# Two buffers for raw weight blocks, conversions stored from their own buffer, gate values turned on TensorE, and larger packets for operands kept in DRAM

## The chip, the cores and the metric

The kernel runs on one core of one Trainium2 chip. The metric is device time in microseconds (us), the median of several executions. All times of single instructions come from one profiled execution.

## What is computed

The reference, cut to what matters here (inputs are float32, the two matrices of the last layer float64):

```python
x = attention(q, k, v, s)          # causal, with a bias from cumsum(max(s, 0)); x is [2304, 512]
P = exp(x @ w_gate - max)          # [2304, 8 experts]
for _ in range(8):                 # rows and columns scaled in turn
    P /= P.sum(1) + 1e-9; P /= P.sum(0) + 1e-9; P *= 2304 / 8
out = 0
for e in range(8):                 # w1[e] is [512, 1024], w2[e] is [1024, 512]
    out += P[:, e:e+1] * (max(x @ w1[e], 0) @ w2[e])
h = out @ w_in                     # w_in is [512, 2048], w_out [2048, 512]
return max(0.01 * h, h) @ w_out
```

## The kernel before

Attention comes first (to about 201 us). The rest is cut into *units*. A unit takes 256 columns of a layer's first matrix and 256 rows of its second for 768 tokens (two blocks of 384, `W = 384`). The tokens make three passes, j = 0, 1, 2. Each pass has 32 units for the 8 experts (4 units an expert), and after the third come three passes of 8 units for the last layer, 120 units in all. In every unit the first product is done by a scheme with seven block products instead of eight: P1 to P7 (function `product`, lines 288 to 290, six matmuls of 384 columns each, since every operand is split into a high and a low part). The order is P1, P6, P5, P7, P2, P4, P3. P1 and P2 go to the PSUM bank that the profile calls FA.

**Pass j = 0** also makes the operands. For unit n, `weights1` loads a raw block of w1 (512 KB) into the tile RAW1 (a part of RB), GpSimd forms four sums of its blocks (SW, also in RB), ScalarE casts to the high parts, GpSimd subtracts to the low parts, all into WQ, of which there are two sets used in turn. `weights2` does the same with a raw block of w2 (tile RAW2), and `sums` forms four sums for later passes in the tile SS. Everything made is stored in DRAM for passes 1 and 2: `w1c` (1792 KB a unit) and `w2s` (1280 KB a unit). In pass 0 the second product of a unit runs plainly (`second`, 36 matmuls of 512 columns), one unit behind the first. VectorE combines the seven products (L956), makes low parts (L984) and adds into `acc` (L1051).

**Passes j = 1, 2 and the last layer** read the made operands back: `fetch1` loads one of the seven blocks of w1c (256 KB) into one of 11 slots, `fetch2` those of w2s, and the second product uses seven products too.

**The conversion** of the float64 matrices (32 blocks, 19 of them in units 4 to 28 of pass 0, in three units of every four; functions `convert`, `conversion`) loads a block into one of two buffers BITS, takes eight VectorE steps (L929 to L936) through the scratch tiles `cva` and `cvb`, and stores `cva` to DRAM (L948). From 1339 us on, `prepare` makes the last layer's operands out of them. **The gate** values P are made by `gating` in the first units; eight stores `pt<-P` (L1086), one per expert, write them to DRAM in the order [expert, token], for passes 1 and 2.

All DMAs are issued by one queue, SyncE's (SP in the profile), in program order: an issue whose wait is open holds everything behind it. The program order of every engine comes from a planner (class `Flow`): every piece of work is entered by `do(engine, key, duration, emit, reads, writes, latency)`, waits follow from the names read and written, and a list schedule with these numbers sets the order. Before, each DMA is entered with 100 ns on SP and a latency of 2500 to 12000 ns.

Of the kernel before, what the change touches and what calls it, by code (L numbers as in the profile page):

```python
# [113 lines left out]
def fused_kernel(ctx: ExitStack, tc: tile.TileContext, q, k, v, s, w_gate, w1, w2, w_in, w_out, out):  # L114
# [110 lines left out]
    def weights1(do, n, key):  # L225
        s = n % 2
        wa, wb = views(n)
        waf = [x.bitcast(F32) for x in wa]
# [1 line left out]
        A = lambda o, k: RAW1[:, 2 * k:2 * k + 2, 128 * o:128 * o + 128]  # L230
        do("sp", key - 0.6, 100, lambda: nc.sync.dma_start(out=RAW1, in_=w1[e][:, 256 * i:256 * i + 256].rearrange("(c p) f -> p c f", p=128)), [], ["raw1"], 3500)
        do("pool", key, pgg(256), sub(SW[:, 0], A(1, 0), A(1, 1), ALU.add), ["raw1"], ["s1"])
        do("pool", key + 0.01, pgg(256), sub(SW[:, 1], SW[:, 0], A(0, 0), ALU.subtract), ["raw1", "s1"], ["s2"])
        do("pool", key + 0.02, pgg(256), sub(SW[:, 2], A(0, 0), A(1, 0), ALU.subtract), ["raw1"], ["s3"])
# [4 lines left out]
        do("act", key + 0.03, pa(256), lambda: nc.scalar.copy(wa[0][:, 6], A(1, 1)), ["raw1"], [("wh6", s)])
        do("act", key + 0.04, pa(1024), lambda: nc.scalar.copy(wa[0][:, 0:4], SW), ss, [("wh0", s)])  # L240
        do("pool", key + 0.04, pgg(512), sub(wa[1][:, 4:6], left, waf[0][:, 4:6], ALU.subtract), ["raw1", ("wh4", s)], [("wl4", s)])
        do("pool", key + 0.05, pgg(256), sub(wa[1][:, 6], A(1, 1), waf[0][:, 6], ALU.subtract), ["raw1", ("wh6", s)], [("wl6", s)])
        do("pool", key + 0.06, pgg(1024), sub(wa[1][:, 0:4], SW, waf[0][:, 0:4], ALU.subtract), ss + [("wh0", s)], [("wl0", s)])

    def weights2(n, key):

# [4 lines left out]
        do("act", key + 0.5, pa(1024), lambda: nc.scalar.copy(wb[0], RAW2), ["raw2"], [("vh", s)])
        do("pool", key + 0.5, pgg(1024), sub(wb[1], RAW2, wb[0].bitcast(F32), ALU.subtract), ["raw2", ("vh", s)], [("vl", s)])
        do("sp", key + 0.9, 100, lambda: nc.sync.dma_start(out=w1c[n], in_=WQ.bitcast(F32)[:, s, 0:2 * NA]), [(x, s) for x in ("wh0", "wl0", "wh4", "wl4", "wh6", "wl6")], [("w1c", n)], 8000)
        for a in range(2):
# [1206 lines left out]
```

## Time and profile before

| | |
|---|---|
| median of 3 runs | 2232.85 us (2225.61 to 2233.7) |
| the profiled execution, its own time | 2235.46 us |
| its span in the profile | 2233.7 us |
| TensorE busy | 2052.5 us, 92% |
| VectorE, GpSimd busy | 1655.9 us, 74%; 1675.0 us, 75% |
| ScalarE busy | 904.0 us, 40% |
| DMA | 518.24 MB in 411474 packets, 106618 of them under 512 B |
| mean granted TensorE clock | 0.972 of full speed |

The shares are means over stages with different limits; the windows by stage, below, tell them apart. PE is TensorE, DVE VectorE, ACT ScalarE, POOL GpSimd. L231 is line 231 of the kernel.

### The profile page before, as it was taken

What the parts mean: (1) busy time and instruction counts of PE and PEld (TensorE: products, weight loads), DVE (VectorE), ACT (ScalarE), POOL (GpSimd) and SP (SyncE); (2) the same over time, 40 slices, a digit from 0 to 9 for tenths busy, and PEclk for the clock granted to TensorE, in tenths of its full rate; (3) what the DMA queues carried; (4) which work ended last, traced back from release to release, by engine and by line L of the source; (5) the groups of instructions that cost most, each with busy time, mean ns of one, the idle gap of its engine ahead of it and who ended that gap; (6) DMA issues with size and microseconds to landing.
All of it is one profiled execution on the core that took longest, in us unless ns stands there. A gap on an engine that the chain in (4) does not pass through costs nothing. (4 is left out here: it accounts for less than half of the span.)

```text
span 2233.7 us, 35592 instructions
## 1 busy us (share of the span) xinstructions
PE 2052.5 (92%) x11471; PEld 1922.6 (86%) x11471; DVE 1655.9 (74%) x2987; ACT 904.0 (40%) x1895; POOL 1675.0 (75%) x1607
## 2 busy tenths in 40 slices
PE   7999967688888799999999999999999999999998
PEld 5786756577777688999999999999999989999997
DVE  6786547466666676889999889788788886776846
ACT  5887312122222223433333344433333344555553
POOL 7789745466666674888888887788777887888885
PEclk9999988899999999999999999999999999999999
DMA  6654768876667667877877779899889977777673
GB/s 148 141 136 127 273 134 195 185 209 244 254 254 263 240 238 274 256 243 248 252 248 248 231 235 286 273 295 296 291 264 292 291 237 254 227 243 214 213 230 99
DMA packets 411474, 518.24 MB, mean 232 GB/s; under 512 B 106618, under 2 KB 298106, under 8 KB 407194
## 3 DMA queue, kind: packets, MB, share of 16 engines
q1 hardware_dynamic: 411290, 515.98, 74.7%
q8 instruction: 92, 1.51, 0.3%
q14 instruction: 92, 0.75, 0.1%
HBM read 362.11 MB, written 144.04 MB: 227 GB/s over the span
## 5 line engine op out<-in xcount | busy, mean ns | idle before, releaser
L288 PE MATMUL sc<-XO,WQ 128*128 128x384 f32 x960 | 333.6, 347 | 78.4 <-DVE HB L984 42.0
L289 PE MATMUL sc<-XO,WQ 128*128 128x384 f32 x960 | 327.5, 341 | 0.0
L290 PE MATMUL sc<-XO,WQ 128*128 128x384 f32 x960 | 326.2, 340 | 0.0
L288 PEld LDWEIGHTS sc<-XO,WQ 128*128 128x128 f32 x960 | 184.9, 193 | 101.2 <-DVE HB L984 45.7
L1229 DVE TENSOR_TENSOR WQ<-WQ 128x512 fp32r<-128x512 f32 x176 | 190.0, 1080 | 58.1 <-ACT WQ L1228 56.9
L267 POOL TENSOR_TENSOR SS<-RAW 128x256 f32<-128x256 f32 x64 | 51.7, 808 | 221.4 <-DMA RAW<-in_moe_w_dram 221.4
L289 PEld LDWEIGHTS sc<-XO,WQ 128*128 128x128 f32 x960 | 184.6, 192 | 4.6
L290 PEld LDWEIGHTS sc<-XO,WQ 128*128 128x128 f32 x960 | 184.6, 192 | 0.0
L1228 ACT CAST WQ<-WQ 128x512 fp32r<-128x512 f32 x176 | 109.2, 620 | 163.8 <-DMA WQ<-w2s 131.6
L1250 DVE TENSOR_TENSOR X<-tr,X 128x384 f32<-128x384 f32 x275 | 149.9, 548 | 33.9 <-PE tr L1244 33.6
L288 PE MATMUL FA<-XO,WQ 128*128 128x384 f32 x480 | 162.5, 339 | 4.5 <-ACT Up L957 2.3
L290 PE MATMUL FA<-XO,WQ 128*128 128x384 f32 x480 | 161.2, 336 | 0.7 <-POOL WQ L223 0.7
L289 PE MATMUL FA<-XO,WQ 128*128 128x384 f32 x480 | 161.4, 336 | 0.0
L956 DVE TENSOR_TENSOR sc<-sc,Uu 128x384 f32<-128x384 f32 x240 | 133.7, 557 | 30.0 <-PE sc L290 29.3
L223 POOL TENSOR_TENSOR WQ<-RB,WQ 128x512 fp32r<-128x512 f32 (+2 forms) x96 | 143.3, 1509 | 4.0 <-ACT WQ L240 2.7
L1211 POOL TENSOR_TENSOR HB<-GG,HB 128x384 fp32r<-128x384 f32 x96 | 107.9, 1127 | 31.0 <-ACT HB L1210 30.9
L956 DVE TENSOR_TENSOR Uu<-FB,Up 128x384 f32<-128x384 f32 x120 | 65.9, 549 | 70.7 <-ACT Up L957 43.8
L929 DVE TENSOR_SCALAR CV<-CV 128x512 uint32<-128x512 uint32 x32 | 25.9, 810 | 113.1 <-DMA win<-CV 107.9
L223 POOL TENSOR_TENSOR RB<-RB 128x256 f32<-128x256 f32 x128 | 94.7, 759 | 17.7 <-DMA RB<-in_moe_w_dram 16.0
L1243 PE MATMUL tr<-HB,WQ 128*128 128x384 f32 x307 | 103.4, 337 | 1.2 <-POOL HB L1211 1.2
L1242 PE MATMUL tr<-HB,WQ 128*128 128x384 f32 x307 | 103.4, 337 | 0.1
L1034 PE MATMUL Y<-WQ,HB 128*128 128x512 f32 x128 | 55.2, 431 | 52.6 <-DVE acc L1051 51.9
(335 smaller groups left out, 6977.4 us busy)
## 6 DMA issues: line engine op xcount, KB each, us to landing
WQ<-w1c SPq DMA_DIRECT2D x616, 256.0 KB
WQ<-w2s SPq DMA_DIRECT2D x440, 256.0 KB
w1c<-WQ SPq DMA_DIRECT2D x32, 1792.0 KB
RB<-in_moe_w_dram SPq DMA_DIRECT2D x32, 512.0 KB
RAW<-in_moe_w_dram SPq DMA_DIRECT2D x32, 512.0 KB
w2s<-WQ SPq DMA_DIRECT2D x64, 256.0 KB
w2s<-SS SPq DMA_DIRECT2D x32, 512.0 KB
CV<-in_moe_w_in_dram SPq DMA_DIRECT2D x16, 512.0 KB
```

The costliest lines, as they stand in the source:

```text
L223: return lambda: nc.gpsimd.tensor_tensor(out=out, in0=x, in1=y, op=op)
L288: nc.tensor.matmul(t, lhsT=hi, rhs=xh, start=new, stop=False, skip_group_check=on)
L289: nc.tensor.matmul(t, lhsT=hi, rhs=xl, start=False, stop=False, skip_group_check=on)
L290: nc.tensor.matmul(t, lhsT=lo, rhs=xh, start=False, stop=(k == 1), skip_group_check=on)
L956: TT = lambda out, x, y: (lambda: v.tensor_tensor(out=out, in0=x, in1=y, op=ALU.add))
L1034: nc.tensor.matmul(y, lhsT=hh, rhs=wb[0][:, f], start=(f == 0), stop=False)
L1211: do(eng, t + 0.02, pgg(W) if eng == "pool" else pq(W), lambda: (nc.gpsimd if eng == "pool" else nc.vector).tensor_tensor(out=OP[k][:, 1], ...
L1228: do("act", t, pa(512), lambda: nc.scalar.copy(hi, lo.bitcast(F32)), [("w2l", k)], [("w2h", k)])
L1229: do(eng, t + 0.05, pgg(512) if eng == "pool" else pd(512), lambda: (nc.gpsimd if eng == "pool" else nc.vector).tensor_tensor(out=lo, in0= ...
L1242: nc.tensor.matmul(y[:, 0:W], lhsT=hi, rhs=oh, start=(x == 0), stop=False)
L1243: nc.tensor.matmul(y[:, 0:W], lhsT=hi, rhs=ol, start=False, stop=False)
L1250: do("dve", t + 0.08, pq(W), lambda: nc.vector.tensor_tensor(out=a, in0=y[:, 0:W], in1=a, op=ALU.add), [yr], [("A", name, s_)])
```

## The change

1. *Raw blocks.* RAW1 and RAW2 become lists of two. The second RAW1 is the upper half of the tile SS, the second RAW2 the start of the tile PB (which holds gate values in later passes). Unit n uses buffer n mod 2, and the loads are entered 0.7 of a unit earlier. SS, before two buffers for `sums`, becomes one.
2. *Conversions.* The last VectorE step writes into the block's own BITS buffer and the store reads from there, so `cva` is free with that step; the buffer's next load waits for the store.
3. *Gate values.* Two TensorE transposes turn P, ScalarE copies the result to SBUF, and two stores write it as [18 tiles, 9, 128 tokens]; the eight stores L1086 go. Loads of PB read three runs of 128 values for each partition in place of one of 384.
4. *Operands in DRAM.* w2s is laid out by pairs of units so that a fetched block is one run in each partition (2 KB, and 4 KB for the new w2d, which holds high and low parts together, in place of 1 KB pieces). The sums' store then writes 1 KB pieces where it wrote 4 KB. The seven blocks of w1c are reordered so that those of P1, P5, P6, P7 stand together: one fetch of 1 MB (8 KB in each partition) into one of two buffers brings them, the other three come alone, each into one buffer of its own.
5. *Planner.* A DMA is entered with 3.2 ns a KB on SP and a latency of 2000 ns (2500 ns for the gate values).

```diff
-    RAW1 = RBw[:, 0:1024].rearrange("p (c f) -> p c f", c=4)
+    RAW1 = [RBw[:, 0:1024].rearrange("p (c f) -> p c f", c=4)]
...
-        do("sp", key - 0.6, 100, lambda: nc.sync.dma_start(out=RAW1, ...), [], ["raw1"], 3500)
+        do("sp", key - 1.3, kb(512), lambda: nc.sync.dma_start(out=raw, ...), [], [r1], 2000)
...
-        do("sp", key - 0.5, 100, lambda: nc.sync.dma_start(out=RAW2, ...), [], ["raw2"], 3500)
+        do("sp", key - 1.2, kb(512), lambda: nc.sync.dma_start(out=raw, ...), [], [r2], 2000)
...
-        sums(do, n, key + 0.6, RAW2, "raw2", SS[:, n % 2], ("ss", n % 2), "pool")
+        sums(do, n, key + 0.6, raw, r2, SS, "ss", "pool")
...
+    RAW2 = [RAWt, PB_.rearrange("p a b n -> p (a b n)")[:, 0:1024].rearrange("p (c f) -> p c f", c=2)]
+    SS = SSt[:, 0:1024].rearrange("p (k f) -> p k f", k=4)
+    RAW1.append(SSt[:, 1024:2048].rearrange("p (c f) -> p c f", c=4))
...
+        def turn():
+            for h in range(2):
+                nc.tensor.transpose(Z[0:half, 128 * h:128 * h + 128], Pf[:, half * h:half * h + half], ident)
+        do("pe", 20, 220, turn, ["P"], ["Z"])
+        do("act", 20, pa(256), lambda: nc.scalar.copy(G[0][0:half, 0:256], Z[0:half, 0:256]), ["Z"], [("g", 0)])
...
-            lambda: v_.tensor_tensor(out=cva.bitcast(F32), in0=cva.bitcast(F32), in1=cvb.bitcast(F32), op=ALU.add),
+            lambda: v_.tensor_tensor(out=bits...[:, 0:512].bitcast(F32), in0=cva.bitcast(F32), in1=cvb.bitcast(F32), op=ALU.add),
...
-        do("sp", key + 0.9, 100, lambda: nc.sync.dma_start(out=dst[...], in_=cva.bitcast(F32)), ["cv"], [(name, m)], 2500)
+        do("sp", key + 0.9, kb(256), lambda: nc.sync.dma_start(out=dst[...], in_=bits...[:, 0:512].bitcast(F32)), [br], [(name, m)], 2000)
...
-    for e in range(E):
-        do("sp", 6, 100, lambda e=e: nc.sync.dma_start(out=pt[e].rearrange("(t p) -> p t", p=128), in_=P[:, :, e]), ["P"], ["pt"], 12000)
...
-    W1R = [WQ[:, 0, 512 * i:512 * i + 512] for i in range(11)]
+    NG = 4
+    W1A = [WQ[:, 0, 512 * NG * i:512 * NG * i + 512 * NG] for i in range(2)]
+    W1B = [WQ[:, 0, 1024 * NG + 512 * i:1024 * NG + 512 * i + 512] for i in range(7 - NG)]
...
-            ev(t - 1.5, lambda k=k1, n=n, name=name, t=t: fetch1(k, n, name, t - 1.5))
+            if PROD[name][1] >= NG:
+                ev(t - 0.8, lambda n=n, o=PROD[name][1], t=t: fetch1(n, o, t - 0.8))
```

The orders below are those of the programs; "waits" names the semaphores that an instruction waits for (DMAHW0 to 7 are DMA landings). First SyncE's queue around one unit of pass 0, before. L253 stores w1c, L250 loads a raw block of w2 (tile RAW2), L231 one of w1 (tile RB), L948 stores a conversion (`win`).

```order
L253 DMA w1c<-WQ 128x3584 [waits DMAHW3_49,Pool_49]
L250 DMA RAW_3063<-in_moe_w_dram 128x2x512 [waits DMAHW4_49,Pool_49]
L260 DMA w2s<-WQ 128x256 [waits DMAHW5_49]
L259 DMA w2s<-WQ 128x2x256 [waits DMAHW6_49]
L231 DMA RB<-in_moe_w_dram 128x4x256 [waits DMAHW7_49,Pool_49]
L260 DMA w2s<-WQ 128x256 [waits DMAHW0_49]
L259 DMA w2s<-WQ 128x2x256 [waits DMAHW1_49,Activation_49]
L948 DMA win_76<-CV 128x512 [waits DMAHW2_49,DVE_49]
L945 DMA CV<-in_moe_w_in_dram 128x1024 [waits DMAHW3_49]
L272 DMA w2s<-SS 128x1024 [waits DMAHW4_49]
L253 DMA w1c<-WQ 128x3584 [waits DMAHW5_49,Pool_49]
```

And in the changed program, where L257, L254, L234, L968 and L277 are those lines' successors and the store of the sums:

```order
L234 DMA SS<-in_moe_w_dram 128x4x256 [waits DMAHW3_49,Pool_49]
L265 DMA w2d<-WQ 128x256
L264 DMA w2d<-WQ 128x2x256 [waits DMAHW5_49,Activation_49]
L257 DMA w1c<-WQ 128x3584 [waits DMAHW6_49,Pool_49]
L265 DMA w2d<-WQ 128x256 [waits DMAHW7_49]
L254 DMA RAW_3064<-in_moe_w_dram 128x2x512 [waits DMAHW0_49,Pool_49]
L264 DMA w2d<-WQ 128x2x256 [waits DMAHW1_49]
L277 DMA w2s<-SS 512x1x256 [waits DMAHW2_49,Pool_49]
L265 DMA w2d<-WQ 128x256 [waits DMAHW3_49]
L234 DMA RB<-in_moe_w_dram 128x4x256 [waits DMAHW4_49,Pool_49]
L968 DMA win_76<-CV 128x512 [waits DMAHW5_49,DVE_49]
```

The raw loads now alternate between the tiles RB and SS, and RAW2 and PB; the wait on GpSimd before each load is still there, but is for the unit two back.

GpSimd's order over one unit of pass 0, before (L267 forms the sums in SS, L223 the rest; a wait on DMAHW before a read of RB or RAW2 is the raw load's landing):

```order
L223 TENSOR_TENSOR WQ<-RB,WQ 128x4x256 [waits PE_49,Activation_49]
L223 TENSOR_TENSOR WQ<-RAW_3063,WQ 128x1024 [waits DMAHW2_49,Activation_49]
L223 TENSOR_TENSOR RB<-RB 128x256 [waits DMAHW7_49,Pool_49]
L223 TENSOR_TENSOR RB<-RB 128x256
L223 TENSOR_TENSOR RB<-RB 128x256 [waits Pool_49] x2
L267 TENSOR_TENSOR SS<-RAW_3063 128x256 [waits DMAHW4_49,DMAHW1_49]
L267 TENSOR_TENSOR SS<-SS,RAW_3063 128x256 [waits Pool_49]
L267 TENSOR_TENSOR SS<-RAW_3063 128x256
L223 TENSOR_TENSOR WQ<-RB,WQ 128x2x256 [waits PE_49,Activation_49]
L267 TENSOR_TENSOR SS<-RAW_3063,SS 128x256 [waits Pool_49]
L223 TENSOR_TENSOR WQ<-RB,WQ 128x256 [waits PE_49,Activation_49]
```

And changed (L272 and L225):

```order
L272 TENSOR_TENSOR SS<-PB,SS 128x256 [waits Pool_49]
L225 TENSOR_TENSOR WQ<-SS,WQ 128x256 [waits PE_49,Activation_49]
L225 TENSOR_TENSOR WQ<-RB,WQ 128x4x256 [waits PE_49,Activation_49]
L225 TENSOR_TENSOR WQ<-RAW_3064,WQ 128x1024 [waits DMAHW5_49,Activation_49]
L225 TENSOR_TENSOR RB<-RB 128x256 [waits DMAHW7_49,Pool_49]
L225 TENSOR_TENSOR RB<-RB 128x256
L225 TENSOR_TENSOR RB<-RB 128x256 [waits Pool_49] x2
L225 TENSOR_TENSOR WQ<-RB,WQ 128x2x256 [waits DMAHW1_49,PE_49,Activation_49]
L272 TENSOR_TENSOR SS<-RAW_3064 128x256 [waits DMAHW5_49,DMAHW0_49]
L225 TENSOR_TENSOR WQ<-RB,WQ 128x256 [waits PE_49,Activation_49]
L272 TENSOR_TENSOR SS<-SS,RAW_3064 128x256 [waits Pool_49]
L272 TENSOR_TENSOR SS<-RAW_3064 128x256
```

The sums L272 now wait for two DMAs, one of them the store of the unit before out of the one SS tile, where it was the store of two units before.

Last, SyncE's queue in pass 1, before (L1182 is `fetch1`, L1223 `fetch2`):

```order
L1182 DMA WQ<-w1c 128x512
L1223 DMA WQ<-w2s 128x2x256 x2
L1182 DMA WQ<-w1c 128x512 x2
L1223 DMA WQ<-w2s 128x2x256 x2
L1182 DMA WQ<-w1c 128x512 x2
L1223 DMA WQ<-w2s 128x2x256 x2
L1182 DMA WQ<-w1c 128x512 x2
```

And changed (L1206 is `fetch1`, L1248 and L1250 `fetch2`):

```order
L1248 DMA WQ<-w2s 128x512 x2
L1206 DMA WQ<-w1c 128x2048
L1250 DMA WQ<-w2d 128x1024
L1206 DMA WQ<-w1c 128x512 x2
L1250 DMA WQ<-w2d 128x1024
L1206 DMA WQ<-w1c 128x512
L1250 DMA WQ<-w2d 128x1024
```

Four of seven single fetches have become one of 2048 columns, and the pairs of `fetch2` one of 1024.

## Rows read from the trace of the kernel before

**Rows 1.** Timeline, TensorE: start, length in us, engine, line, operation, tiles.

```profile
552.00 0.33 PE L288 MATMUL FA<-XO,WQ 128*128 128x384 f32 x1
...
567.64 0.33 PE L288 MATMUL FA<-XO,WQ 128*128 128x384 f32 x1
```

**Rows 2.** Busy time by stage: us, busy (count) by engine, clock, DMA share, GB/s.

```profile
201.40:301.20 99.80, 92.69 (x514) 75.89 (x513) 60.59 (x147) 40.87 (x77) 75.78 (x77) 0.97 0.69 235
301.20:490.40 189.20, 126.37 (x547) 109.64 (x546) 94.06 (x153) 36.91 (x65) 92.53 (x85) 0.85 0.82 182
490.40:816.40 326.00, 278.45 (x1327) 243.42 (x1326) 213.23 (x353) 85.54 (x151) 216.20 (x201) 0.96 0.67 247
816.40:872.20 55.80, 50.15 (x235) 44.14 (x234) 41.20 (x58) 17.83 (x30) 36.23 (x30) 0.94 0.74 273
872.20:1338.80 466.60, 464.88 (x2666) 460.30 (x2665) 417.42 (x666) 172.31 (x341) 388.93 (x344) 1.00 0.78 245
1338.80:1838.40 499.60, 478.91 (x2690) 471.38 (x2689) 412.60 (x682) 192.34 (x373) 395.88 (x354) 0.99 0.88 282
1838.40:2233.70 395.30, 378.29 (x2173) 373.27 (x2171) 264.56 (x391) 202.69 (x419) 309.89 (x280) 0.99 0.68 210
```

**Rows 3.** Busy time by stretch, units 4, 20, 21 and 28 alone.

```profile
285.40:301.20 15.80, 15.80 (x82) 14.23 (x81) 14.43 (x26) 5.08 (x9) 7.71 (x6) 1.00 0.73 201
...
643.60:662.10 18.50, 15.91 (x79) 14.00 (x78) 13.45 (x19) 3.53 (x8) 12.07 (x11) 1.00 0.71 263
...
662.10:688.10 26.00, 17.77 (x80) 15.18 (x79) 13.09 (x26) 6.27 (x11) 13.75 (x14) 0.87 0.63 235
...
800.50:816.40 15.90, 15.88 (x79) 13.99 (x78) 11.24 (x17) 3.43 (x7) 10.71 (x9) 1.00 0.66 240
```

**Rows 4.** Waits of SyncE's queue, 201.4 to 872.2 us: total, times, longest.

```profile
SPq L231 <- POOL WQ L223: 297.0, 31, 13.7
```

**Rows 5.** Timeline, SyncE's queue (a start is when an issue went out).

```profile
659.98 1.22 SPq L259 DMA_DIRECT2D w2s<-WQ  x1
...
670.86 0.38 SPq L231 DMA_DIRECT2D RB<-in_moe_w_dram  x1
...
672.37 0.46 SPq L948 DMA_DIRECT2D win<-CV  x1
...
675.54 0.67 SPq L250 DMA_DIRECT2D RAW<-in_moe_w_dram  x1
```

**Rows 6.** Timeline, VectorE; in brackets idle time before and what ended it.

```profile
662.90 0.67 DVE L936 TENSOR_TENSOR CV<-CV 128x512 f32<-128x512 f32 x1
...
679.02 0.43 DVE L929 TENSOR_SCALAR CV<-CV 128x512 uint32<-128x512 uint32 x1 [10.61 <-DMA win<-CV]
```

**Rows 7.** Timeline, GpSimd.

```profile
686.48 0.86 POOL L267 TENSOR_TENSOR SS<-RAW 128x256 f32<-128x256 f32 x1 [8.13 <-DMA RAW<-in_moe_w_dram]
```

**Rows 8.** Waits of the engines, 201.4 to 872.2 us.

```profile
POOL SS L267 <- DMA RAW<-in_moe_w_dram: 221.4, 29, 17.6
...
DVE CV L929 <- DMA win<-CV: 107.9, 12, 20.8
```

**Rows 9.** Timeline, SyncE's queue, around one store of gate values.

```profile
315.99 0.51 SPq L1086 DMA_DIRECT2D pt<-P  x1
...
331.38 0.37 SPq L259 DMA_DIRECT2D w2s<-WQ  x1
```

**Rows 10.** A conversion's fifth step: ns min/median/max, 500 to 620 us.

```profile
L933 DVE TENSOR_TENSOR CV<-CV x5: 681/681/2775, 499.3 to 604.9; 128x512 uint32<-128x512 uint32 x5
```

**Rows 11.** The same step grouped, 552 to 872 us: busy us, mean ns.

```profile
L933 DVE TENSOR_TENSOR CV<-CV 128x512 uint32<-128x512 uint32 x10 | 13.5, 1347 | 0.1
```

**Rows 12.** Waits of the engines, 1339 to 1838 us.

```profile
DVE CV L267 <- DMA CV<-wout: 15.1, 7, 3.4
...
DVE CV L1328 <- DMA CV<-win: 13.6, 7, 3.4
...
PE sc L288 <- DVE Uu L956: 12.7, 10, 2.6
```

More of the change, by code (lines that the diff above doesn't have):

```diff
@@ L229, in weights1 @@
         e, i = divmod(n, 4)
[L230 to L234, printed above, removed]
@@ L241, in weights1 @@
-        do("pool", key + 0.04, pgg(512), sub(wa[1][:, 4:6], left, waf[0][:, 4:6], ALU.subtract), ["raw1", ("wh4", s)], [("wl4", s)])
-        do("pool", key + 0.05, pgg(256), sub(wa[1][:, 6], A(1, 1), waf[0][:, 6], ALU.subtract), ["raw1", ("wh6", s)], [("wl6", s)])
-        do("pool", key + 0.06, pgg(1024), sub(wa[1][:, 0:4], SW, waf[0][:, 0:4], ALU.subtract), ss + [("wh0", s)], [("wl0", s)])
+        raw, r1 = RAW1[s], ("raw1", s)
+        A = lambda o, k: raw[:, 2 * k:2 * k + 2, 128 * o:128 * o + 128]
@@ new lines, in weights1 @@
+        ss = ["s1", "s2", "s3", "s4"]
+        left = raw[:, :, 0:128].rearrange("p (o k) f -> p o k f", o=2)
+        do("act", key + 0.02, pa(512), lambda: nc.scalar.copy(wa[0][:, 0:6:5], left), [r1], [("wh4", s)])
+        do("act", key + 0.03, pa(256), lambda: nc.scalar.copy(wa[0][:, 6], A(1, 1)), [r1], [("wh6", s)])
+        do("act", key + 0.04, pa(1024), lambda: nc.scalar.copy(wa[0][:, 1:5], SW), ss, [("wh0", s)])
+        do("pool", key + 0.04, pgg(512), sub(wa[1][:, 0:6:5], left, waf[0][:, 0:6:5], ALU.subtract), [r1, ("wh4", s)], [("wl4", s)])
@@ L823, in fused_kernel @@
     place("cv", ("CV", 2048, 3072))
-    place("raw1", ("RB", 0, 1024))
+    place("ss", ("SS", 0, 1024))
+    place(("raw1", 0), ("RB", 0, 1024))
+    place(("raw1", 1), ("SS", 1024, 2048))
+    place(("raw2", 0), ("RAW2", 0, 1024))
+    place(("raw2", 1), ("PB", 0, 1024))
     for i in range(4):
@@ L827, in fused_kernel @@
         place(("g", i), ("GG", W * i, W * i + W))
-    place("raw2", ("RAW2", 0, 1024))
     for i in range(8):
@@ L915, in gating @@
             do("dve", -1, 1100, cols_, [], ["P", "Z"], far)
+        half = NTT // 2 * (E + 1)
+        def turn():
[3 more added lines that the diff above has]
+        do("act", 20, pa(256), lambda: nc.scalar.copy(G[0][0:half, 0:256], Z[0:half, 0:256]), ["Z"], [("g", 0)])
+        for h in range(2):
+            do("sp", 20, 100, lambda h=h: nc.sync.dma_start(out=pt[NTT // 2 * h:NTT // 2 * h + NTT // 2].rearrange("t e n -> (t e) n"), in_=G[0][0:half, 128 * h:128 * h + 128]), [("g", 0)], ["pt"], 2500)
     def convert(bits):
@@ L1067, in second @@
                 if sub == 2:
-                    do("sp", key + 0.1, 100, lambda half=half: nc.sync.dma_start(out=xd[j][:, :, half, :], in_=X[:, :, HALF * half + W * j:HALF * half + W * j + W]),
-                       [("xo", 9 * half + 3 * j + x) for x in range(3)], [("xd", j, half)], 4000)
+                    do("sp", key + 0.1, kb(768), lambda half=half: nc.sync.dma_start(out=xd[j][:, :, half, :], in_=X[:, :, HALF * half + W * j:HALF * half + W * j + W]),
+                       [("xo", 9 * half + 3 * j + x) for x in range(3)], [("xd", j, half)], 2000)
     CONVS = {4 + n: 1 for n in range(25) if n % 4 != 3}
@@ L1219, in fetch2 @@
         kind, j, u, ci = unit(n)
-        k, rd = q % 5, [("w2s", ci), ("w2s", ci + 1)]
-        for a in ((1,) if PART[name] < 4 else (0, 1)):
-            part = PART[name] + (3 * a if PART[name] >= 4 else 0)
-            do("sp", t, 100, lambda a=a, part=part: nc.sync.dma_start(out=W2R[k].bitcast(F32)[:, a], in_=w2s[ci:ci + 2, :, part, :].rearrange("x p c -> p x c")), rd, [("w2" + "hl"[a], k)], 3000)
+        k, part = q % 5, PART[name]
+        to, names = W2R[k].bitcast(F32), [("w2h", k), ("w2l", k)]
+        if part < 4:
+            do("sp", t, kb(256), lambda: nc.sync.dma_start(out=to[:, 1], in_=w2s[ci // 2][:, part]), [("w2s", ci), ("w2s", ci + 1)], names[1:], 2000)
+        else:
+            do("sp", t, kb(512), lambda: nc.sync.dma_start(out=to, in_=w2d[ci // 2][:, part - 4]), [("w2d", ci), ("w2d", ci + 1)], names, 2000)
     def round2(q, t, eng):
```

117 lines of the change are left out of this document (64 added, 53 removed).

## Prediction, made before the changed kernel was run

> **What bounds the kernel now.** I read the timeline of TensorE first, to cut the time into units: a dense unit of pass 0 starts its P1 at 552.00 and the next one's comes at 567.64 [rows 1], so such a unit costs 15.64 us. The windows by stage then show where units are longer [rows 2]. Pass 0 has 32 units in 201.4 to 872.2, 670.8 us, against 32 x 15.64 = 500.5 if all were dense: 170.3 too many. By stretch: units 0 to 4 (99.80 us) 21.6, units 5 to 11 (189.20) 79.7, units 12 to 28 (326.00) 60.1, units 29 to 31 (55.80) 8.9. Pass 1 has no such excess (466.60 us of which TensorE is busy 464.88); pass 2 takes 33.0 more than pass 1 and shows TensorE 20.7 us idle. So a gain has to come from pass 0, above all from units 5 to 28, 139.8 us. There the clock also falls, to 0.85 in the mean of units 5 to 11 and to 0.87 in unit 21, alone [rows 2, 3]; unit 20 with 2.6 us of idle time kept 1.00.
>
> Next the waits, to see what makes these units long. SyncE's queue stands in pass 0 for 297.0 us in 31 waits at L231, where the load of raw w1 waits for GpSimd to be done with RAW1 [rows 4]. All that is behind it in the queue stands too. One case in unit 21's neighbourhood: nothing goes out from 661.2 to 670.86, where the raw load is released; the conversion's store behind it goes out at 672.37 [rows 5], though the sum L936 that it stores had started at 662.90 and took 0.67 us; VectorE, whose next conversion must overwrite `cva`, stands 10.61 us and starts at 679.02 [rows 6], that is when the store has landed, 6.6 us after its issue. VectorE's other work, which TensorE needs, is behind that step in program order. GpSimd in turn waits for the raw load of w2, issued late at 675.54 and used at 686.48, 10.9 us after [rows 5, 7]. In all GpSimd waits 221.4 us for these loads and VectorE 107.9 us for conversion stores [rows 8]. So three engines wait in a ring: load for GpSimd, store behind the load, VectorE for the store, TensorE for VectorE.
>
> In units 5 to 11 a second cause lies on top: a store of one expert's gate values, whose 4-byte pieces keep the queue busy. After the one issued at 315.99 the next issue but one is at 331.38 [rows 9].
>
> **The change, part by part.** *Raw buffers and the conversions' own store.* With two raw buffers the load of unit n waits for GpSimd's use of unit n-2, and that is over long before in a queue that is at most a unit ahead; the store leaves from BITS, so VectorE's first step waits for no store. What is then left of the excess in a conversion's unit? Three units show a conversion without a store wait: 4 (15.80 us), 28 (15.90) and 20 (18.50) [rows 3], so 0.16, 0.26 and 2.86 above dense, 1.1 in the mean. Of units 5 to 28, 18 have a conversion. I take the mean, 18 x 1.1 = 19.8; the bounds are 18 x 0.2 = 3.6 and 18 x 2.86 = 51.5. The gain is so 139.8 - 19.8 = 120 us (88.3 to 136.2). It includes the gate stores' part, since no 4-byte store is left.
>
> Could another engine refuse 15.64 us? GpSimd is busy 216.20 us in the 17 units 12 to 28, 12.7 a unit or 81% of 15.64. The DMA engines are busy 0.67 of these 326 us, 12.8 a unit or 0.82 of 15.64, and the trace has a stage with 0.88 [rows 2]. VectorE has 213.23/17 = 12.5. All fit, none with much room.
>
> *VectorE against GpSimd.* Why unit 20 is slow without a store wait matters for the sum. A conversion's fifth step takes 681 ns in the median and up to 2775 [rows 10], with a mean of 1347 ns from 552 on [rows 11]; GpSimd was 12.07 us busy in unit 20, but 7.71 in unit 4 and 10.71 in unit 28 [rows 3]. So it is held while GpSimd works, and in the changed kernel GpSimd works in more of each unit's time (81% where it is now 216.20/326.00 = 66%). That is inside the bounds above; by the ratio 1.22 on the 0.67 us by which the mean stands above 681, one such step would lose 0.15 more, 18 times 2.6 us. The Trainium skill ("SBUF — State Buffer", section "SBUF: two separate sides") says that VectorE and GpSimd share a port pair as an exclusive lock, and that a VectorE instruction with two SBUF operands and a GpSimd one that reads SBUF shut each other out for a whole instruction. By that rule a busier GpSimd costs VectorE more in every such unit, which is the first rival below; the trace agrees in the one slow step (681 to 2775 ns), and doesn't show that every unit pays.
>
> *Units 0 to 4 and 29 to 31* keep their 21.6 and 8.9: the first stand in the attention's tail, the last at the change of pass, and no edit touches what they do.
>
> *The turn of the gate values.* Two transposes, about as two more matmuls: 78 in 15.64 us, 0.2 us each, so +0.4, and a ScalarE copy that lies beside them. I take +0.5. Two stores replace eight.
>
> *Packets and fetch order.* Bytes don't change, pieces of fetched w2s grow from 1 to 2 or 4 KB and those of the sums' store shrink from 4 to 1 KB. Pass 1 has nothing to gain. In pass 2 VectorE waits 15.1 and 13.6 us for loads of the last layer's preparation and TensorE 12.7 us for VectorE [rows 12]; the bounds are 0 and the 20.7 us of idle time. I take a quarter of TensorE's own 12.7, 3 us, nearer to nothing, since the same bytes have to come in.
>
> Sum, against the profiled execution's own 2235.46 us: 2235.5 - 120 - 3 + 0.5 = 2113. That execution is 2.6 us above the median, so the forecast is **2110 us**.
>
> **The rivals.** *VectorE is held in every conversion's unit.* All 18 are like unit 20: 51.5 in place of 19.8, so 2142. For it speaks that GpSimd will be busier than in unit 20's 12.07 of 18.50 us, against it units 4 and 28.
>
> *The single tile SS.* The sums of unit n now wait for the store of unit n-1. Four sums take 4 x 0.86 us [rows 7] = 3.4, so a unit of 15.64 leaves 12.2 for that store to land. Landings here were 6.6 (256 KB) and 10.9 us (512 KB in a full queue), the store is 512 KB in 1 KB pieces. At 14 us each of 24 units gets 1.8 longer: +43, 2153.
>
> *The queue still stands.* If the entries 0.7 of a unit earlier put the loads so far ahead that they still wait for GpSimd, only the gate stores' part goes: units 5 to 11 would cost as the units 12 to 28 do, 60.1/17 = 3.5 each above dense, 24.7 instead of 79.7. Gain 55: about 2175.
>
> *All of pass 0 dense.* 136.2 from units 5 to 28, also the 8.9 of units 29 to 31, half of pass 2's idle time (10.4): 2235.5 - 136.2 - 8.9 - 10.4 + 0.5 - 2.6 = 2078.
>
> *Slower: the fetches of passes 1 and 2 and the last layer starve TensorE.* Before, 11 slots in turn held seven blocks; now three blocks have one buffer each. Such a buffer is free only when its product has run and is wanted again six products of seven later: 14.58 us (466.60/32) x 6/7 = 12.5 us. While a fetch lands sooner than that nothing is lost, and both landings above are shorter, though in a stage with less traffic. Beyond it all 88 units (32 + 32 + 24) get longer; the gain of 122 is used up at 1.4 us a unit, so at a landing of 13.9. At 15 us, 88 x 2.5 = 220: 2330.
>
> **How the numbers follow.** Likeliest, with its own range of 2092 to 2125: 0.55. VectorE held: 0.18. SS: 0.06. Queue still standing: 0.05. All dense: 0.10. Starved fetches: 0.06, of which I give 0.02 to landings that just eat up the gain. The range 2080 to 2155 reaches from just above the dense case to just above the SS case, and leaves out the queue, the fetches and half of the dense case: 0.16. Half a per cent, some 11 us, is about what a measurement of this kernel can tell from no change; all cases but the starved fetches lie far on the faster side: faster 0.94, same 0.02, slower 0.04.
>
> **What would show it.** Right: SyncE's wait of 297.0 at the raw load and VectorE's 107.9 for a conversion's store are gone or below 30; GpSimd's 221.4 for raw loads has shrunk to a few us a unit or to waits for other things; units 5 to 28 take 15.6 to 17 us each, so 201 to 872 becomes some 550 us; clock 1.00 there; passes 1 and 2 as long as before. VectorE held: units with conversions near 18.5 and a mean of the fifth step near 2 us, with TensorE waiting for VectorE. SS: GpSimd's sums wait for their own store. The queue: L231's successor (L234) still has long waits on GpSimd. Starved: TensorE waits in pass 1 for fetches of w1c. The prediction is wrong if a step that the trace of before doesn't show sets the pace at 15.64: above all a landing in pass 0 at a DMA share of 0.82, or any stall in the stages that are dense now.

## The result, and the profile of the changed kernel

The changed kernel takes 2095.92 us in the median of four runs, the kernel before 2229.23 us beside it: a ratio of 0.9405, with a 95% interval of 0.9379 to 0.9431. Forecast were 2110 us.

The profiled execution has a span of 2097.3 us. The windows by stage, cut at the same units as [rows 2] (units 0 to 4, 5 to 11, 12 to 28, 29 to 31, pass 1, pass 2, last layer; columns as there):

```profile
200.10:300.00 99.90, 91.67 (x512) 75.15 (x511) 59.90 (x147) 39.99 (x76) 81.94 (x85) 0.98 0.76 266
300.00:416.90 116.90, 112.72 (x550) 99.52 (x549) 105.90 (x154) 37.62 (x66) 94.60 (x84) 0.99 0.83 287
416.90:687.20 270.30, 267.01 (x1328) 238.86 (x1327) 246.30 (x358) 87.71 (x153) 231.65 (x206) 1.00 0.87 302
687.20:735.00 47.80, 47.23 (x236) 42.15 (x235) 38.99 (x56) 17.57 (x30) 28.28 (x20) 1.00 0.66 232
735.00:1198.80 463.80, 463.32 (x2665) 460.42 (x2664) 416.83 (x662) 172.80 (x342) 389.26 (x344) 1.00 0.74 247
1198.80:1700.60 501.80, 478.12 (x2691) 471.51 (x2690) 424.84 (x679) 192.71 (x372) 394.65 (x354) 0.99 0.84 280
1700.60:2097.30 396.70, 379.72 (x2173) 374.86 (x2171) 262.03 (x394) 202.71 (x420) 308.43 (x280) 0.98 0.64 211
```

Against [rows 2], units 0 to 4 take 99.90 us where they took 99.80, units 5 to 11 116.90 (189.20), units 12 to 28 270.30 (326.00), units 29 to 31 47.80 (55.80). Pass 0 so gives 72.3 + 55.7 + 8.0 - 0.1 = 135.9 of the 136.4 us by which the span fell. Pass 1 is 2.8 shorter, pass 2 2.2 and the last layer 1.4 longer. The granted clock in units 5 to 28 is 0.99 and 1.00 of full speed, so nearly always the upper of its two levels (2.4 GHz); before it was 0.85 and 0.96.

Units 20 and 21 alone, which answer to [rows 3]:

```profile
544.10:559.80 15.70, 15.70 (x80) 14.10 (x79) 15.38 (x21) 4.21 (x9) 14.85 (x14) 1.00 0.77 269
559.80:576.60 16.80, 15.91 (x80) 13.97 (x79) 16.77 (x24) 5.62 (x10) 13.39 (x13) 1.00 0.84 296
```

Unit 20 is dense. Unit 21 is 1.2 us longer, and there VectorE is busy 16.77 of 16.80 us: it is now the bound in one unit of four (13, 17, 21 and 25 take 16.6 to 16.8 us).

The waits of SyncE's queue in pass 0, for [rows 4]:

```profile
SPq L234 <- POOL WQ L225: 102.4, 28, 7.6
SPq L277 <- POOL SS L272: 54.8, 25, 7.3
```

The queue still stands: 102.4 us at the raw load of w1 (L234) and 54.8 at the sums' store (L277). The waits of the engines in the same stretch, for [rows 8]:

```profile
POOL SS L272 <- DMA w2s<-SS: 15.5, 9, 4.6
...
POOL SS L272 <- DMA PB<-in_moe_w_dram: 6.7, 3, 4.0
```

GpSimd's 221.4 us for raw loads have gone down to single cases, and VectorE has no wait for a conversion's store left. The one tile SS costs GpSimd 15.5 us in all.

Two of a conversion's steps have become longer. By line and form on VectorE, units 4 to 28, the first two steps and the fifth (the last numbers: busy us, mean ns, idle us):

```profile
L950 DVE TENSOR_SCALAR CV<-CV 128x512 f32<-128x512 f32 x19 | 30.9, 1627 | 0.2
...
L949 DVE TENSOR_SCALAR CV<-CV 128x512 uint32<-128x512 uint32 x19 | 26.9, 1414 | 0.0
L953 DVE TENSOR_TENSOR CV<-CV 128x512 uint32<-128x512 uint32 x19 | 17.7, 930 | 0.2
```

And the same three steps in the kernel before, units 4 to 28:

```profile
L933 DVE TENSOR_TENSOR CV<-CV 128x512 uint32<-128x512 uint32 x19 | 23.7, 1250 | 0.2
...
L929 DVE TENSOR_SCALAR CV<-CV 128x512 uint32<-128x512 uint32 x19 | 11.8, 619 | 113.1 <-DMA win<-CV 107.9 <-DMA wout<-CV 5.2
...
L930 DVE TENSOR_SCALAR CV<-CV 128x512 f32<-128x512 f32 x19 | 10.4, 547 | 0.2
```

They went from 619 and 547 ns to 1414 and 1627. The means of all eight add up to 8.26 us a conversion where they were 6.12. What they wait for is in the trace of the changed kernel: one second step in unit 21, and the GpSimd instruction that runs when it starts.

```profile
563.44 2.56 POOL L225 TENSOR_TENSOR WQ<-PB,WQ 128x1024 fp32r<-128x1024 f32 x1
564.62 1.67 DVE L950 TENSOR_SCALAR CV<-CV 128x512 f32<-128x512 f32 x1
```

GpSimd ends at 566.00, the step at 566.29. In units 4 to 28 of the changed kernel 37 of the 38 first and second steps start while a GpSimd instruction runs and end 0.27 to 0.29 us after it. In the kernel before, 25 of the 38 had no GpSimd instruction beside them and took 0.41 to 0.43 us.

### The profile page after: what moved, and what is told of

Same layout as the page of the kernel before. It is cut to its first block, busy times and chain, and to the rows that moved or that the text cites. A ratio compares the mean times of both kernels' runs of the same rounds, so it can differ in the third digit from the quotient of the medians.

```text
span 2097.3 us, 34707 instructions
## 1 busy us (share of the span) xinstructions
PE 2020.6 (96%) x11473; PEld 1904.9 (91%) x11473; DVE 1706.9 (81%) x2987; ACT 906.4 (43%) x1896; POOL 1689.2 (81%) x1607
## 5 line engine op out<-in xcount | busy, mean ns | idle before, releaser
L294 PE MATMUL sc<-XO,WQ 128*128 128x384 f32 x960 | 328.3, 342 | 29.7 <-DVE Uu L976 21.6
L295 PE MATMUL sc<-XO,WQ 128*128 128x384 f32 x960 | 323.8, 337 | 0.0
L296 PE MATMUL sc<-XO,WQ 128*128 128x384 f32 x960 | 323.0, 337 | 0.0
L294 PEld LDWEIGHTS sc<-XO,WQ 128*128 128x128 f32 x960 | 181.6, 189 | 46.7 <-DVE Uu L976 27.6
L295 PEld LDWEIGHTS sc<-XO,WQ 128*128 128x128 f32 x960 | 182.0, 190 | 4.6
L296 PEld LDWEIGHTS sc<-XO,WQ 128*128 128x128 f32 x960 | 182.0, 190 | 0.0
L976 DVE TENSOR_TENSOR sc<-sc,Uu 128x384 f32<-128x384 f32 x240 | 133.7, 557 | 32.4 <-PE sc L296 31.2
L225 POOL TENSOR_TENSOR WQ<-RB,WQ 128x512 fp32r<-128x512 f32 (+1 forms) x64 | 113.8, 1786 | 28.4 <-ACT WQ L243 17.8
L1270 PE MATMUL tr<-HB,WQ 128*128 128x384 f32 x307 | 103.1, 336 | 1.2 <-POOL HB L1236 1.2
L1269 PE MATMUL tr<-HB,WQ 128*128 128x384 f32 x307 | 103.1, 336 | 0.1
L1271 PE MATMUL tr<-HB,WQ 128*128 128x384 f32 x307 | 103.0, 335 | 0.0
L1003 ACT ACTIVATE HB<-FB 128x384 fp32r<-128x384 f32 x32 | 15.8, 493 | 201.2 <-DVE FB L976 201.2
L1056 PE MATMUL tr<-WQ,HB 128*128 128x512 f32 x256 | 101.8, 398 | 0.0
L1055 PE MATMUL tr<-WQ,HB 128*128 128x512 f32 x256 | 101.5, 397 | 0.0
L1054 PE MATMUL tr<-WQ,HB 128*128 128x512 f32 x256 | 100.2, 391 | 0.0
```

The source lines that it names most:

```text
L225: return lambda: nc.gpsimd.tensor_tensor(out=out, in0=x, in1=y, op=op)
L294: nc.tensor.matmul(t, lhsT=hi, rhs=xh, start=new, stop=False, skip_group_check=on)
L295: nc.tensor.matmul(t, lhsT=hi, rhs=xl, start=False, stop=False, skip_group_check=on)
L296: nc.tensor.matmul(t, lhsT=lo, rhs=xh, start=False, stop=(k == 1), skip_group_check=on)
L976: TT = lambda out, x, y: (lambda: v.tensor_tensor(out=out, in0=x, in1=y, op=ALU.add))
L1269: nc.tensor.matmul(y[:, 0:W], lhsT=hi, rhs=oh, start=(x == 0), stop=False)
```

## The experiments

Twelve kernels ran, each beside the kernel before. A ratio is always to the kernel before in the same job; its medians there were 2237.1, 2235.7 and 2242.2 us, so ratios are compared and not times. First four that take one part out of the changed kernel.

**gate_back**: the eight stores of gate values are back.

```diff
-        do("pe", 20, 220, turn, ["P"], ["Z"])
...
+    for e in range(E):
+        do("sp", 6, 100, lambda e=e: nc.sync.dma_start(out=pt[e].rearrange("(t p) -> p t", p=128), in_=P[:, :, e]), ["P"], ["pt"], 12000)
```

> The changed kernel with the eight stores of gate values in 4-byte pieces back, all else as changed (2096). Ring theory with gate stores on top: the stores keep the queue busy on their own, two raw buffers or not, so units 5 to 11 lose again what they lost above the rhythm of units 12 to 28, about 55 us: 2150, with units near 40 us. Rival (the double buffers cover a late queue): at most 10 us, 2106.

0.9694 (0.9662 to 0.9725), 2.9% of before or 65 us more than the changed kernel. SyncE's queue around one gate store, and the windows of units 5 to 11 and 12 to 28:

```profile
313.37 0.46 SPq L1096 DMA_DIRECT2D pt<-P  x1
313.88 6.16 SPq L264 DMA_DIRECT2D w2d<-WQ  x1
```

```profile
299.50:464.50 165.00, 127.44 (x547) 110.33 (x546) 93.96 (x153) 35.50 (x63) 79.54 (x73) 0.83 0.95 179
464.50:747.20 282.70, 271.98 (x1328) 241.71 (x1327) 248.03 (x358) 88.93 (x154) 244.39 (x218) 0.98 0.87 304
```

The issue behind the store takes 6.16 us by itself, the DMA engines are 0.95 busy in units 5 to 11 and move 179 GB/s, where the changed kernel moves 287 at 0.83. This stretch is 48.1 us longer than in the changed kernel, and units 12 to 28 are 12.4 longer. The second raw buffers don't cover these stores.

**cva_store**: conversions stored from the scratch tile.

```diff
-            lambda: v_.tensor_tensor(out=bits...[:, 0:512].bitcast(F32), in0=cva..., in1=cvb..., op=ALU.add),
+            lambda: v_.tensor_tensor(out=cva.bitcast(F32), in0=cva..., in1=cvb..., op=ALU.add),
...
-        do("sp", key + 0.9, kb(256), lambda: ...(out=dst[...], in_=bits...), [br], [(name, m)], 2000)
+        do("sp", key + 0.9, kb(256), lambda: ...(out=dst[...], in_=cva.bitcast(F32)), ["cv"], [(name, m)], 2000)
```

> The changed kernel with the conversions stored from the scratch tile again. Ring theory: the queue is free now, the store goes out within about 1 us and lands 6.6 us later, while the next conversion's first step comes 1.5 us after the last step when two units in a row convert; about 12 such pairs of units lose some 5 us each: +60, 2156, with VectorE waiting for the store. Rival (the late queue alone made that wait): under +10, 2106, because the planner moves the steps apart.

0.9519 (0.9495 to 0.9542): some 25 us lost, between the two theories. VectorE's timeline at one conversion, then the windows:

```profile
404.36 0.52 DVE L949 TENSOR_SCALAR CV<-CV 128x512 uint32<-128x512 uint32 x1 [3.56 <-DMA win<-CV]
...
406.56 2.62 DVE L952 TENSOR_SCALAR CV<-CV 128x512 uint32<-128x512 uint32 x1
409.21 2.71 DVE L953 TENSOR_TENSOR CV<-CV 128x512 uint32<-128x512 uint32 x1
...
413.84 0.55 DVE L976 TENSOR_TENSOR sc<-sc,Uu 128x384 f32<-128x384 f32 x1
```

```profile
300.80:429.20 128.40, 116.28 (x549) 101.92 (x548) 106.08 (x153) 37.97 (x66) 98.08 (x89) 0.95 0.78 274
429.20:718.50 289.30, 274.46 (x1327) 242.44 (x1326) 244.39 (x358) 88.74 (x153) 229.13 (x202) 0.98 0.79 277
```

VectorE waits at most 3.56 us for a store, not 5 and more; what follows in this conversion is two steps of 2.62 and 2.71 us. Units 5 to 28 lose 30.5 us, and five of them hold the loss: units 11, 15, 19, 23 and 27 take 24.5, 24.1, 21.0, 19.8 and 20.4 us, dense ones in the changed kernel. In unit 11, shown here, VectorE waits and then runs seven steps of the conversion in a row, 404.36 to 413.84, before the next combining of products (L976), and TensorE stands 6.25 us until 414.97. Unit 15 shows the same. So the price there is a short wait and a program order that puts work for TensorE behind a whole conversion.

**one_raw**: one buffer for each raw block, loads entered as late as before, SS double again.

```diff
-        raw, r1 = RAW1[s], ("raw1", s)
+        raw, r1 = RAW1[0], ("raw1", 0)
...
-        do("sp", key - 1.3, kb(512), ...
+        do("sp", key - 0.6, kb(512), ...
```

> The changed kernel with one buffer each for RAW1 and RAW2, their loads entered where they were before, and two for the sums. Ring theory: SyncE's queue stands at the raw loads again for over 200 us and GpSimd waits for them; VectorE doesn't wait for a store, so that conversion units cost what unit 20 of before did, 2 to 3 us above dense: +40 to +60, 2136 to 2156. Rival (the store's own buffer is enough): under +10, 2106.

0.9388 (0.9372 to 0.9404): nothing lost. The queue stands more than in the changed kernel, and the stretch of units 12 to 28 (first row of the windows; the second is pass 1) is 2 us longer:

```profile
SPq L234 <- POOL WQ L225: 130.1, 29, 8.3
```

```profile
416.20:688.50 272.30, 268.81 (x1327) 238.32 (x1326) 251.56 (x356) 85.78 (x152) 230.05 (x206) 0.95 0.87 302
737.40:1201.40 464.00, 463.22 (x2666) 460.53 (x2665) 412.39 (x662) 171.24 (x340) 389.57 (x344) 0.95 0.74 247
```

This speaks against my ring as I had told it: with everything else changed, the second raw buffers are worth nothing.

**old_packets**: layout in DRAM and fetches as before, the other four parts as changed.

```diff
-    W1A = [WQ[:, 0, 512 * NG * i:512 * NG * i + 512 * NG] for i in range(2)]
-    W1B = [WQ[:, 0, 1024 * NG + 512 * i:1024 * NG + 512 * i + 512] for i in range(7 - NG)]
+    W1R = [WQ[:, 0, 512 * i:512 * i + 512] for i in range(11)]
```

> The changed kernel with the operands in DRAM laid out and fetched as before (256 KB fetches in 1 KB pieces, 11 slots), all else as changed. Ring theory: bytes and dense stages are the same, so within 5 us of 2096. Rival (bigger packets made part of the gain, by freeing DMA time in pass 0 or passes 1 and 2): 2110 or more, with the excess in pass 2 larger by 10 us or more.

0.9347 (0.9325 to 0.9369), the lowest but one of all. Windows of pass 1, pass 2 and the last layer:

```profile
738.30:1206.00 467.70, 464.40 (x2666) 460.26 (x2665) 418.65 (x663) 171.99 (x340) 388.97 (x344) 1.00 0.80 247
1206.00:1700.10 494.10, 474.65 (x2689) 468.24 (x2688) 424.69 (x682) 193.58 (x374) 397.09 (x355) 0.99 0.89 285
1700.10:2094.80 394.70, 379.77 (x2173) 374.21 (x2172) 263.40 (x391) 202.93 (x418) 309.40 (x279) 0.99 0.69 211
```

The large packets save 3.9 us in pass 1 (463.80 against 467.70) and cost 7.7 in pass 2 and 2.0 in the last layer: 5.8 us on the wrong side, about what can still be told. It repeats, though: from the start of pass 1 to the end, the five kernels with the new packets and the new planner's numbers take 1360.6 to 1363.6 us, the three with the old packets and the new numbers (old_packets, and planner_alone and own_gate_planner below) 1352.4 to 1356.5.

So the gate stores stood, the second buffers fell, and the ring was in doubt. Two theories were left. A: buffers, own store and gate stores are the gain, and the planner's numbers follow them. B: the numbers themselves, which set the order in the queue, did what the second buffers were thought to do.

Next the planner's numbers out of the changed kernel, and single parts put into the kernel before.

**old_planner**: every DMA at 100 ns and the latencies of before, all other parts changed.

```diff
-        do("sp", key - 1.3, kb(512), ..., [r1], 2000)
+        do("sp", key - 1.3, 100, ..., [r1], 3500)
...
-        do("sp", key + 0.9, kb(1430), ..., [("w1c", n)], 2000)
+        do("sp", key + 0.9, 100, ..., [("w1c", n)], 8000)
```

> The changed kernel with every DMA entered in the planner at 100 ns and with the latencies of before. Theory A (buffers and gate stores are the gain, the planner's numbers only follow them): within 10 us of the changed kernel, 0.94 of before. Theory B (the numbers did what the second raw buffers were thought to do, since one buffer cost nothing: they put steps that must wait far enough apart): 0.95 of before or more, 20 us or more lost in units 5 to 28.

0.9678 (0.9646 to 0.971): 2.7% lost, the second largest loss. Waits of SyncE's queue and of GpSimd in pass 0:

```profile
SPq L277 <- POOL SS L272: 230.7, 30, 10.1
```

```profile
POOL SS L272 <- DMA PB<-in_moe_w_dram: 70.3, 14, 6.2
POOL SS L272 <- DMA RAW<-in_moe_w_dram: 60.6, 14, 7.3
```

Now the sums' store (L277) stands at the head, 7.7 us a time, and the raw loads are behind it; GpSimd waits 131 us for them. Units 12 to 28 take 312.8 us and pass 2 513.8 (270.3 and 501.8 in the changed kernel).

**gate_alone**: the kernel before with the gate values turned (the reverse of the diff of gate_back).

> The kernel before with the gate values turned on TensorE and nothing else. Ring theory: units 5 to 11 come down to the rhythm of units 12 to 28, 55 us: 0.975 of before, and VectorE still waits some 100 us for conversion stores. Rival (the gate stores cost 65 as they did when put back into the changed kernel): 0.970.

0.972 (0.9681 to 0.976). Units 5 to 11 and 12 to 28:

```profile
301.60:431.80 130.20, 115.19 (x550) 100.52 (x549) 96.48 (x153) 37.45 (x66) 91.27 (x82) 0.97 0.71 255
431.80:761.20 329.40, 286.44 (x1327) 250.49 (x1326) 217.30 (x358) 87.32 (x153) 219.38 (x203) 0.94 0.67 249
```

59.0 us gone from units 5 to 11 and none from units 12 to 28: the two causes are apart in place too.

**own_alone**: the kernel before with conversions stored from their own buffer (the reverse of cva_store).

> The kernel before with conversions stored from their own buffer and nothing else. Theory A (the store is the link of the ring that matters, raw buffers are not): units 13, 17, 21, 25 fall from 26 us to 16 to 18.5, others by 1 or so; in units 5 to 28 the gain is 50 to 70 us: 0.97 of before, with the queue still standing some 200 us at the raw load. Rival (the late queue hits GpSimd's loads as hard): 0.985 or more.

0.9984 (0.9969 to 1.0): nothing. Waits of the engines and of the queue:

```profile
POOL SS L267 <- DMA RAW<-in_moe_w_dram: 210.6, 29, 21.1
```

```profile
SPq L231 <- POOL WQ L223: 264.4, 31, 13.9
SPq L945 <- DMA win<-CV: 57.3, 16, 13.5
```

VectorE's 107.9 us for stores are gone. But the queue still stands 264.4 us at the raw load, and has a new wait: the next load into a conversion's buffer now waits in the queue for the store out of it (L945, 57.3 us). GpSimd still waits 210.6 us for raw loads (221.4 before), and ScalarE 76.3 us at L251 (29.4 before). Units 12 to 28 take 323.6 us.

**raw_alone**: the kernel before with two raw buffers, one SS, loads 0.7 of a unit earlier (the reverse of one_raw).

> The kernel before with two raw buffers each, their loads entered 0.7 of a unit earlier, and one tile for the sums, nothing else. Ring theory as predicted: the store behind the load goes out at once, VectorE's wait falls from 10.6 to about 2 us: 60 us of the excess go, 0.972 of before. Theory A (the link is the scratch tile, the load only one of several that hold the queue): under 25 us, 0.99 of before.

0.9681 (0.9655 to 0.9707). The queue's waits, then the windows:

```profile
SPq L252 <- POOL SS L269: 178.8, 25, 13.8
SPq L232 <- POOL WQ L223: 58.1, 29, 10.6
```

```profile
300.50:483.50 183.00, 124.38 (x548) 107.63 (x547) 94.80 (x153) 36.94 (x65) 90.94 (x85) 0.81 0.88 189
483.50:754.40 270.90, 269.02 (x1328) 238.08 (x1327) 230.07 (x356) 85.56 (x153) 230.69 (x204) 1.00 0.84 301
```

The wait at the raw load of w1 (L232) falls from 297.0 to 58.1 us, and units 12 to 28 from 326.00 to 270.90, as short as in the changed kernel, though the queue stands 178.8 us at the load of w2 (L252): that load is for a unit ahead, and nothing behind it seems to be wanted soon. VectorE's wait for stores in these units falls from 57.7 to 15.2 us. Units 5 to 11, under the gate stores, win 6.2 us alone. The second buffers and the earlier entry of the loads came together here; which of the two counts wasn't tried.

**raw_and_gate**: raw_alone and gate_alone together.

> The kernel before with two raw buffers each (one tile for the sums) and the gate values turned, nothing else: conversions stored from the scratch tile, old packets, old planner's numbers. Theory A (two independent causes): the gains of gate_alone (0.972) and raw_alone (0.968) add up, 0.940, the whole of the change; units 12 to 28 near 271 us, units 5 to 11 near 120. Theory B (the rest of the change is needed for the end of it): 0.955 or more, with VectorE's wait for conversion stores above 60 us.

0.937 (0.934 to 0.940): the whole gain of the change, by two parts of five. The windows, and VectorE's wait for stores:

```profile
302.60:417.80 115.20, 111.28 (x550) 98.19 (x549) 100.19 (x153) 37.37 (x66) 93.50 (x83) 1.00 0.81 291
417.80:689.30 271.50, 269.01 (x1327) 238.04 (x1326) 232.31 (x357) 86.03 (x153) 232.37 (x206) 1.00 0.84 300
```

```profile
DVE CV L945 <- DMA win<-CV: 22.3, 10, 4.3
```

**planner_alone**: the kernel before with the planner's new numbers (the reverse of old_planner).

> The kernel before with the planner's new numbers for DMAs and nothing else (the eight gate stores stay at 100 and 12000 ns). Theory A (the numbers only follow the buffers): within 1% of before, with some 300 us of standing at the raw load. Theory B (the numbers take the raw load out of the way as the second buffers do, which is why one_raw cost nothing): units 12 to 28 fall from 326 to 275-290 us, 0.975 to 0.985 of before, the 4-byte stores still holding units 5 to 11.

0.968 (0.9643 to 0.9718): as much as the raw buffers alone. The queue near the place of [rows 5]:

```profile
654.91 1.23 SPq L949 DMA_DIRECT2D win<-CV  x1
...
657.52 1.32 SPq L260 DMA_DIRECT2D w2s<-WQ  x1
664.39 0.38 SPq L232 DMA_DIRECT2D RB<-in_moe_w_dram  x1
```

```profile
DVE CV L930 <- DMA win<-CV: 30.2, 9, 9.5
```

The queue stands here too, 657.52 to 664.39, at a raw load with one buffer. But the conversion's store (654.91) is now ahead of that load and not behind it, and VectorE's wait for stores is 30.2 us in place of 107.9. The new order did more than move this store: GpSimd's wait for raw loads of w2 fell too, from 221.4 to 99.4 us. Units 12 to 28 take 287.40 us (326.00 before, 270.90 in raw_alone), units 5 to 11, with the gate stores, 175.30; 9 us more come from the stages behind pass 0. So the numbers match the raw buffers in the total, and not stage by stage.

**own_gate_planner**: own store, gate turned, new numbers; neither raw buffers nor packets.

> Conversions stored from their own buffer, gate values turned, the planner's new numbers; one raw buffer each, two tiles for the sums, old packets and 11 slots. Theory B (numbers and own store do without raw buffers, and the new packets cost 5 us): 0.933 to 0.937 of before, faster than the changed kernel by 5 to 12 us. Theory A: 0.95 or more, since one_raw's result needed the new packets.

0.9365 (0.9341 to 0.939). With the queue standing twice as long as in the changed kernel:

```profile
SPq L232 <- POOL WQ L224: 208.0, 31, 9.5
```

it is as fast as the changed kernel; whether it is faster (0.9365 against 0.9405, overlapping) this can't tell. Of the kernels that do all the work none beats the changed one by more than 0.6%.

**no_sums**: the changed kernel without GpSimd's sums after unit 0.

```diff
+        if eng == "dve" or n == 0:
-        do(eng, key, d_, op(to[:, 0], A(1, 0), A(1, 1), ALU.add), [rr], [name])
+            do(eng, key, d_, op(to[:, 0], A(1, 0), A(1, 1), ALU.add), [rr], [name])
...
```

> The changed kernel without GpSimd's four sums of w2 in units 1 to 31 of pass 0 (the stores go out as before, with the sums of unit 0; the results of passes 1 and 2 are not the reference's). VectorE held by GpSimd: the eight steps of a conversion, 8.26 us now and 4.10 by the shortest of each, hold 4.16 us with GpSimd busy 86% in units 12 to 28; at 12.9 - 3.5 us a unit (62%) the hold falls to about 3.0 and the sum to 7.1; units 13, 17, 21, 25 go from 16.8 to 15.7, 2087 to 2092. Rival (the steps' length has nothing to do with GpSimd): 8.2 us as now and 16.8 us in these units.

0.9332 (0.9308 to 0.9356). Units 12 to 28, and the first two steps of a conversion:

```profile
416.00:681.90 265.90, 265.90 (x1327) 239.02 (x1326) 238.98 (x358) 88.01 (x153) 174.47 (x136) 1.00 0.78 271
```

```profile
L951 DVE TENSOR_SCALAR CV<-CV 128x512 f32<-128x512 f32 x19 | 29.5, 1554 | 0.2
L950 DVE TENSOR_SCALAR CV<-CV 128x512 uint32<-128x512 uint32 x19 | 22.1, 1166 | 0.0
```

265.90 us is 17 times 15.64: every unit is dense. The eight steps add up to 7.62 us, GpSimd busy 174.47 of 265.90 (66%, 86% in the changed kernel). So the direction is that of a VectorE held by GpSimd, and the size about half of what was expected (0.64 us less instead of 1.2). GpSimd's share of busy time isn't the measure: in raw_and_gate it is busy 232.37 of 271.50 us, 86% as in the changed kernel, and the eight steps add up to 7.28 us, less than here. What counts is which GpSimd instruction runs when a step starts. Leaving the sums out also frees GpSimd and the queue, so this alone doesn't part the two effects on the unit's length.

## Why the prediction came out, and where it did not

The total was 2110 against 2096, and the place was right: units 5 to 28 gave 128.0 us where 120 were forecast (bounds 88.3 to 136.2).

*Gate stores.* Told as a second cause and sized at 55 us in the rival of the standing queue: 59.0 in units 5 to 11 alone (gate_alone), 48.1 there when put back (gate_back). Shown. The prediction misread [rows 9]: seven issues lie between the two rows, not one. The eighth, at 331.38, had waited 8.6 us for the gate store issued at 315.99 to land, some 15 us after its issue; in the orders shown above every eighth issue waits on the same landing semaphore. So the queue is held by the landing of such a store, eight issues on.

*The ring.* "three engines wait in a ring: load for GpSimd, store behind the load, VectorE for the store" holds in the kernel before: with the load standing less (raw_alone) or the store moved ahead of it (planner_alone) VectorE's wait for stores in units 12 to 28 falls from 57.7 us to 15.2 and 6.0, and these units get 55.1 and 38.6 us shorter. What failed is a credit: the step gave the gain to raw buffers **and** the store's own buffer. The own store alone was worth nothing, since the wait only changed its engine, from VectorE to the queue (57.3 us before the next load into the buffer); the section on the change names this wait, and the prediction didn't follow it. In the changed kernel it is worth some 25 us, while raw_and_gate does without it although VectorE waits as long for stores there (22.3 us, 19.4 in cva_store). So its worth there hangs on the program order that the planner makes, as cva_store's unit 11 shows. The total didn't show the wrong credit, since all parts were in the changed kernel: that much is luck.

*The planner's numbers* had no term at all. They are another way to open the ring, as large as the raw buffers in the total (0.968 both), so that one of the two could be left out unnoticed (one_raw, own_gate_planner). Left out of the whole change they cost 2.7%, though raw_and_gate runs at 0.937 with the old ones. So own store and new packets together, under the old numbers, cost about 3%, with the sums' store at the head of the queue; which of the two does it wasn't tried. Of the 69.7 us between the profiles of old_planner and raw_and_gate 19.7 lie behind pass 0.

*The sign to look for* was wrong: a wait at the raw load below 30 us. It is 102.4, and 208.0 in a version as fast. Standing time of the queue is no measure; what stands behind is.

*What is left in a conversion's unit*: forecast 19.8 us, measured 11.8 in units 5 to 28 (387.2 less 24 x 15.64). Of these, 7.4 lie in units 5 to 7 (54.3 us), where VectorE is busy 49.0 us and the cause stays open, and 4.4 in units 13, 17, 21 and 25, where VectorE is the bound. Here VectorE against GpSimd was the term. I had looked at the fifth step, priced it by GpSimd's share of busy time, and expected 0.15 us more of it; that step became shorter (1250 to 930 ns over these units, [rows 11] show 1347), while the first two, with one operand from SBUF, grew by 0.8 and 1.1 us. The Trainium skill ("SBUF — State Buffer", section "Who interferes with whom") counts VectorE's `tensor_scalar`, the form of these two steps, among those that can enter a two-port mode and then contend with GpSimd; the trace of the changed kernel agrees with it (37 of 38 such steps end 0.27 to 0.29 us after the GpSimd instruction beside them, 1414 and 1627 ns in the mean where they took 619 and 547), and shows 2.1 us more of VectorE in each conversion. The rival "VectorE is held in every conversion's unit" is so right in the mechanism and wrong in the price: most units had just room for it (unit 20: 15.38 of 15.70 us).

*The one tile SS*, a rival at +43 us, costs GpSimd 15.5 us of waits in pass 0. In raw_and_gate it costs 46.3, and units 12 to 28 are as short there (271.50 us), so it is off the path.

*Units 29 to 31* gave 8.0 us that I had left in place; raw_alone takes 7.5 of them, so they too belonged to the queue.

*Packets*: forecast -3, measured +0.8 in the three later stages against before, +5.8 against old_packets. The slower rival, starved fetches, did not come: TensorE is busy 463.32 of 463.80 us in pass 1 with single buffers.

## What to carry to other kernels

When a queue in program order stands at a wait, ask what is behind it and who needs that soonest; here another order of the issues was worth as much as second buffers (0.968 both). Before crediting a change of several parts, look for two that open the same wait, since taking out either then shows nothing, and follow each buffer that is freed to the instruction that now waits for it. The stores in 4-byte pieces were a cause of their own here, which the second raw buffers didn't cover. And an engine's lengthened step is read from what runs beside it when it starts, not from the other engine's share of busy time.

## Not expected of the hardware

In the profile of one_raw the granted clock is 0.95 through pass 1, where that of the changed kernel is 1.00, yet pass 1 takes 464.00 us against 463.80. No stretch of 50 us in its trace shows more than 0.95, and its three other executions have means of 0.988 to 0.991 at nearly the same time. A clock some hundredths lower in the record doesn't have to show in the time; why it was lower stays open.
